# A fused attention, gated convolution and channel mix: reciprocals straight from PSUM for two pairs of six, and weights and vectors prepared at other places

## The chip, the core and the metric

One NeuronCore of one Trainium2 chip runs the kernel as one program. The metric is the device time of an execution in microseconds (us).

## What is computed

The batch is 4, there are 12 heads of 64, 448 positions, and the model width is 768. Three blocks follow each other:

```python
# attention with soft-capped scores
scores = cap * np.tanh(scale * np.matmul(q, k.transpose(0, 1, 3, 2)) / cap)
attn = np.exp(scores - max); attn = attn / (attn.sum(-1) + 1e-09)
x = np.matmul(attn, v)                        # then heads side by side: (4, 448, 768)
# gated causal convolution, 5 taps per channel
gate = 1 / (1 + np.exp(-gate_pre))            # gate_pre: sum of conv_w[k] * x shifted by k
x = gate * (x @ w_val) @ w_out
# channel mix
k = np.maximum(xk @ w_k, 0); v = k * k @ w_v  # xk, xr: x mixed with x one position before
out = 1 / (1 + np.exp(-(xr @ w_r))) * v
```

q, k, v, cap, mu_k and mu_r are float32; w_val, w_out, w_k, w_v, w_r and conv_w arrive as 64-bit floats.

## The kernel before

The work is cut by batch and by pair of heads. Two heads fill the 128 partitions, so there are 24 pairs, pair i being pair i % 6 of batch i // 6. Activations lie with channels on partitions and positions along the row (128 x 448). Each dense product is done in three matmuls: both operands are split into a high part and a remainder (`split_hi`, `split_lo`), and high x high, high x low and low x high are added in PSUM.

A pair goes through six pieces (`piece`): piece 0 makes two score tiles, their tanh and exp (`scores`, `exps`) and has GpSimd start adding up the exponentials (`add_up`); piece 1 multiplies the exponentials of the pair before with v (`pv`); pieces 2 and 3 turn q and k of the next pair (`qk_T`); piece 4 makes the other score tiles; piece 5 sums the exponentials of the pair before over the keys with a matmul against ones (`sums`, L294).

The sums have to be inverted and multiplied onto the pair's result `x_f`. In `sums`, ScalarE copies them out of PSUM (L296), a DMA spreads them over 128 partitions (7 columns), VectorE adds a small guard and inverts (`invert`, L300 and L301), a DMA writes them to DRAM, and `prep` loads them back as a full tile R (128 x 448, `load_R`). GpSimd multiplies (`divide`, L369). Then `prep` runs the five taps of the convolution over `x_f` (first tap on ScalarE L379, the other four on VectorE L385), and after the last pair of a batch a sigmoid over the whole gate (L389).

These steps are not issued at once. A clock of steps counts pieces and dense halves; `post(n, fn)` has fn issued n steps later. So the order of every engine's queue is written out by hand, and `in_order` keeps it:

```python
        post(2, lambda: dma(out=r, in_=rows[0::64]))
        post(4, invert)
        post(6, lambda: dma(out=rec_d[i]..., in_=r))
            post(8, load_R)
            post(11, divide)
            at(13 + k, tap, k)
            at(13 + TAPS, sigmoid)
```

All DMAs are issued by SyncE in the order of the program.

The weights arrive as 64-bit floats. `w_fetch` loads a unit (128 output columns), `narrow` makes 32-bit floats of it (one step on ScalarE, four on VectorE: L445 to L448), and `w_make` splits a half unit (three 128 x 128 blocks) into its two parts, and stores them to DRAM for the batches that follow. `w_ready` has the parts of the half four further on (LA = 4) loaded, or made if nobody made them before. The buffers of raw weights (tags x64 and wr) are two each.

The program has these stages. First, FIRST = 10 pairs run their pieces alone, with all six units of w_val narrowed between them (MAKE_IN = 46 is the tick by which they are to be done; units 3, 4, 5 and 0, 1 are split too). `vectors`, called ahead of pair 1, loads conv_w, mu_k and mu_r, narrows conv_w in five steps on VectorE and turns them with TensorE (L666) into per-channel columns. Then the layers val and out of batches 0 to 3 run (`first_stage`), each of six outputs in two halves of nine matmuls (`layer`, L631). Behind each half, `behind_first` issues pieces of the remaining pairs at a pace of 1.55 pieces a half in batches 0 and 1 and 3.0 after that; there, too, w_out's units are narrowed (batch 0) and w_r's (batch 1), and the x of the next batch is split (SPLIT_AT, `x_split`). In batch 3 and after it w_k and w_v are made resident, and r, k and v of all batches follow (`second_stage`). Behind all this stands a branch for a large cap, which these inputs don't take.

Of the kernel before, what the change touches and what calls it, by code (L numbers as in the profile page):

```python
# [8 lines left out]
F32 = mybir.dt.float32  # L9
F32R = mybir.dt.float32r  # L10
I32 = mybir.dt.int32
I64 = mybir.dt.int64
ACTF = mybir.ActivationFunctionType
ALU = mybir.AluOpType
# [2 lines left out]
DRAM = bass.MemoryType.DRAM  # L17


FIRST = 10  # L20

MAKE_IN = 46

PACE = (1.55, 1.55, 3.0)

SPLIT_AT = (14, 15, 16, 21, 22, 23)

# [6 lines left out]
LA = 4  # L34
# [12 lines left out]
def attention_gated_conv_channel_mix_kernel(  # L47
# [27 lines left out]
    nc = tc.nc  # L75
    B, H, S, D = q.shape
# [3 lines left out]
    NP = H // 2  # L80
# [60 lines left out]
    def dma(**kw):  # L141
        nc.sync.dma_start(**kw)  # L142
# [15 lines left out]
    def post(n, fn, *args):  # L158
        due.setdefault(steps[0] + n, []).append((fn, args))
# [30 lines left out]
    def load_v(i):  # L190
        b, hp = divmod(i, NP)
        vn = pools["raw"].tile([128, J, D], F32, tag="vn", name="vn")
        dma(
            out=vn,
            in_=v[b, 2 * hp:2 * hp + 2].rearrange("h s d -> (h s) d").rearrange("(j p) d -> p j d", p=128),
        )
        v_t[i] = (vn, vz[i % 2])
# [92 lines left out]
    def sums(i):  # L290
        acc = acc_t.pop(i)
        ps = ps_m.tile([128, S], F32, tag="sum", name="sum")
        for h in range(2):
            nc.tensor.matmul(ps[64 * h:64 * h + 64], lhsT=ones, rhs=acc[:, h], start=True, stop=True)  # L294
        rows = pools["x"].tile([128, S], F32, tag="xs", name="rows", bufs=1)
        nc.scalar.copy(rows, ps)  # L296
        r = pools["x"].tile([128, NS], F32, tag="rec", name="rec")

        def invert():
            nc.vector.tensor_scalar(r, r, guard, None, ALU.add)  # L300
            nc.vector.reciprocal(r, r)  # L301

        post(2, lambda: dma(out=r, in_=rows[0::64]))
        post(4, invert)
        post(6, lambda: dma(out=rec_d[i].rearrange("h s -> (h s)").rearrange("(p n) -> p n", n=NS), in_=r))
        prep(*divmod(i, NP))

    def shifted(i):
# [45 lines left out]


    again = [False]
    x_f, x_R, x_blk, gate_t, gated = {}, {}, {}, {}, set()

    def prep(b, hp):

        i = b * NP + hp
        at = (lambda t, fn, *args: fn(*args)) if again[0] else post

        def load_R():
            x_R[i] = pools["x"].tile([128, S], F32, tag="R", name="R")
            dma(out=x_R[i], in_=rec_d[i].unsqueeze(1).to_broadcast([2, 64, S]))

        def divide():
            nc.gpsimd.tensor_tensor(x_f[i], x_f[i], x_R.pop(i), ALU.mult)  # L369

        def tap(k):
            if hp == 0 and k == 0:
                gp = gr_p if b % 2 else pools["x"]
                gate_t[b] = gp.tile([128, KD, S], F32, tag="gr", name="gate", bufs=1)
            x, g = x_f[i], gate_t[b][:, hp]
            eng = turn(GATE[b], hp)
            w = vecT[:, hp, TAPS - 1 - k:TAPS - k]
            if k == 0:
                nc.scalar.activation(out=g, in_=x, func=ACTF.Copy, scale=w)  # L379
            elif eng is nc.gpsimd:  # L380
                y = pools["x"].tile([128, S], F32, tag="tap", name="tap", bufs=1)
                eng.tensor_scalar(y[:, k:], x[:, :S - k], w, 1.0, ALU.mult, ALU.mult)
                eng.tensor_tensor(g[:, k:], g[:, k:], y[:, k:], ALU.add)
            else:
                eng.scalar_tensor_tensor(g[:, k:], x[:, :S - k], w, g[:, k:], ALU.mult, ALU.add)  # L385

        def sigmoid():
            ga = gate_t[b].rearrange("p k s -> p (k s)")
            nc.scalar.activation(out=ga, in_=ga, func=ACTF.Sigmoid)  # L389
            gated.add((b, again[0]))  # L390

        if not again[0]:
            post(8, load_R)
            post(11, divide)
        if again[0] or b == 0:
            at(14, x_split, b, hp)
        for k in range(TAPS):
            at(13 + k, tap, k)
        if hp == KD - 1:
            at(13 + TAPS, sigmoid)  # L400

    def new_blk():
        return blk_p.tile([128, 2, S], F32R, tag="blk", name="blk")
# [1 line left out]
    def split_blk(src, hi_eng, lo_eng, wait=0):  # L405
        t = new_blk()
        split_hi(hi_eng, t[:, 0], src)
        if wait:
            post(wait, split_lo, lo_eng, t[:, 1], src, t[:, 0])
        else:  # L410
            split_lo(lo_eng, t[:, 1], src, t[:, 0])
        return t[:, 0], t[:, 1]

    def x_split(b, hp):
        x_blk[b, hp] = split_blk(x_f[b * NP + hp], nc.scalar, engines["PD"[hp % 2]], 0 if again[0] else 1)


# [232 lines left out]
                pend.append((b, o))  # L650

    def vectors():
        vec = pools["mk"].tile([128, DM], F32, tag="wr", name="vec")[0:8]
        if conv_w.dtype == I64:
            c64 = pools["mk"].tile([128, DM, 2], I32, tag="x64", name="c64")
            dma(out=c64[0:TAPS].rearrange("p n two -> p (n two)"), in_=conv_w.bitcast(I32))
        else:
            dma(out=vec[0:TAPS], in_=conv_w)
        dma(out=vec[TAPS:TAPS + 1], in_=mu_k.unsqueeze(0))
        dma(out=vec[TAPS + 1:TAPS + 2], in_=mu_r.unsqueeze(0))  # L660
        if conv_w.dtype == I64:
            for fn in narrow(c64[0:TAPS], vec[0:TAPS]):
                fn()
        pc = ps_m.tile([128, KD, 8], F32, tag="sum", name="pc")
        for o in range(KD):
            nc.tensor.transpose(  # L666
                pc[:, o, :TAPS + 2], vec[:TAPS + 2, o * 128:(o + 1) * 128], ident[:TAPS + 2, :TAPS + 2]
            )
        nc.vector.tensor_copy(vecT[:, :, :TAPS + 2], pc[:, :, :TAPS + 2])
        nc.vector.tensor_scalar(mu1, vecT[:, :, TAPS:TAPS + 2], -1.0, 1.0, ALU.mult, ALU.add)  # L670


    stage = ExitStack()
# [2 lines left out]
    dma(out=cap_c, in_=cap.to_broadcast([128, 1]))  # L676
    load_qk(1)
    load_v(0)
    make_identity(nc, ident)
    for p in prev:  # L680
        nc.vector.memset(p[:, 0:1], 0.0)
# [52 lines left out]

    first = len(nc.cur_bb.bb.instructions)
    ops = []
    order = (3, 4, 5, 0, 1, 2)[:KD]

    def make_val(j):
        o = order[j]  # L740
        ops.extend(w_wide("val", o, "ADDDD"))
        if j + 1 < len(order):
            w_fetch("val", order[j + 1])
        for a in range(2):
            if j < 3:
                ops.append(lambda a=a: w_make("val", o, a, nc.vector))
            elif 2 * o + a < LA:
                ops.append(lambda a=a: w_spl.update({2 * o + a: w_make("val", o, a, nc.vector)}))
        if j < 3:
            made.add(("val", o))  # L750
        if j + 1 < len(order):
            ops.append(lambda: make_val(j + 1))

    make_val(0)
    n_ops, n_done, ticks = 8 * len(order), 0, 0
    for i in range(FIRST):
        if i == 1:
            vectors()
        for p in pieces(i):
            piece(*p)  # L760
            ticks += 1
            while ops and n_done * MAKE_IN < ticks * n_ops:
                ops.pop(0)()
                n_done += 1
            step()
    while ops:
        ops.pop(0)()
    dense_from[0] = 0


# [4 lines left out]
    def behind_first(b):  # L775
        def behind(n):
            credit[0] += PACE[min(b, len(PACE) - 1)]
            while todo and credit[0] >= 1:
                piece(*todo.pop(0))
                credit[0] -= 1  # L780
                step()
            u = n // 2

            if b == 0 and KD <= u + 3 < 2 * KD:
                if n % 2 == 0:
                    wide.extend(w_wide("out", u + 3 - KD, "ADDDD"))
                    if u + 4 < 2 * KD:
                        w_fetch("out", u + 4 - KD)
                for _ in range(1 if n % 2 == 0 else len(wide)):
                    if wide:  # L790
                        wide.pop(0)()
            if b == 1 and u // 2 < KD:
                o = u // 2
                if n % 4 == 0:
                    wide.extend(w_wide("r", o, "ADDDD"))
                    if o + 1 < KD:
                        w_fetch("r", o + 1)
                if n % 4 < 2:
                    for _ in range(1 if n % 2 == 0 else len(wide)):
                        if wide:  # L800
                            wide.pop(0)()
                else:
                    w_make("r", o, n % 4 - 2, (nc.gpsimd, nc.vector)[n % 2])
                    made.add(("r", o))
            if b == B - 1:
                if n + 1 in XR_AT0:
                    mixed(0, XR_AT0.index(n + 1), 1)
                return lambda: res_step("val")
            elif n + 1 in SPLIT_AT and not again[0]:
                x_split(b + 1, SPLIT_AT.index(n + 1))  # L810
        return behind
# [100 lines left out]
```

## Time and profile before

| | |
|---|---|
| median of 3 runs | 879.13 us (877.95 to 880.84) |
| the profiled execution, its own time | 877.56 us |
| its span, from first to last instruction | 875.8 us |
| TensorE busy (mean granted clock 0.938) | 752.7 us, 86% of the span |
| VectorE, ScalarE, GpSimd busy | 480.0, 443.1, 343.6 us |

The profile is of one execution. PE is TensorE, DVE VectorE, ACT ScalarE, POOL GpSimd, SP SyncE, whose queue issues the DMAs. In the granted clock 1.00 is 2.4 GHz and 0.5 is 1.2 GHz. Idle time in front of an instruction is given with what ended it (`<-`). An engine takes its instructions strictly in order, so what stands behind a waiting instruction waits too. L631 is line 631 of the kernel. TensorE's busy time contains matmuls at half clock and gaps in the pipeline, so it isn't the least time that its work needs.

### The profile page before, as it was taken

What the parts mean: (1) busy time and instruction counts of PE and PEld (TensorE: products, weight loads), DVE (VectorE), ACT (ScalarE), POOL (GpSimd) and SP (SyncE); (2) the same over time, 40 slices, a digit from 0 to 9 for tenths busy, and PEclk for the clock granted to TensorE, in tenths of its full rate; (3) what the DMA queues carried; (4) which work ended last, traced back from release to release, by engine and by line L of the source; (5) the groups of instructions that cost most, each with busy time, mean ns of one, the idle gap of its engine ahead of it and who ended that gap; (6) DMA issues with size and microseconds to landing.
All of it is one profiled execution on the core that took longest, in us unless ns stands there. A gap on an engine that the chain in (4) does not pass through costs nothing.

```text
span 875.8 us, 10699 instructions
## 1 busy us (share of the span) xinstructions
PE 752.7 (86%) x3798; PEld 583.8 (67%) x3798; DVE 480.0 (55%) x653; ACT 443.1 (51%) x673; POOL 343.6 (39%) x259
## 2 busy tenths in 40 slices
PE   3676689869789898779899977888999999999996
PEld 2333345536456655545789756768999999999995
DVE  3577887759945746464525756886423332333310
ACT  4475869647575757676232445543443343335311
POOL 2296777636744636576023646774000000000000
PEclk8687879979889999999989999999999999999999
DMA  7264533564647577754668898333720390145001
GB/s 177 66 178 133 148 91 90 140 192 146 205 154 242 182 206 231 236 166 130 209 219 305 292 311 302 108 118 99 229 74 21 85 286 15 43 124 168 1 21 47
DMA packets 148029, 135.50 MB, mean 155 GB/s; under 512 B 78071, under 2 KB 127223, under 8 KB 147966
## 3 DMA queue, kind: packets, MB, share of 16 engines
q1 hardware_dynamic: 147966, 134.72, 51.4%
q8 instruction: 32, 0.52, 0.2%
q14 instruction: 31, 0.25, 0.1%
HBM read 109.35 MB, written 25.25 MB: 154 GB/s over the span
## 4 chain that ended last, share of the span: by engine, by line
PE 45%; DVE 16%; DMA 16%; ACT 10%; issue 6%; POOL 4%; SPq 2%; POOLq 0%; ACTq 0%; DVEq 0%
PE psd L631 37%; PE pv L286 3%; DMA rec<-rows 3%; DVE wr L447 3%; DMA recd<-rec 3%; PE s L244 3%; DVE gate L385 3%; ACT t L246 2%; DVE wr L446 2%; ACT t L253 2%; SPq L142 2%; DMA of<-out 2%; DVE wr L448 1%; DMA wp<-pdout 1%; DMA R<-recd 1%
## 5 line engine op out<-in xcount | busy, mean ns | idle before, releaser
L631 PE MATMUL psd<-blk,wp 128*128 128x448 f32 x1296 | 292.3, 381 | 20.9 <-ACT r L568 6.3
L631 PEld LDWEIGHTS psd<-blk,wp 128*128 128x128 f32 x1296 | 246.6, 194 | 66.5 <-issue 21.3
L631 PE MATMUL psd<-blk,wv 128*128 128x448 f32 x576 | 124.6, 372 | 1.3 <-ACT blk L170 1.1
L170 ACT CAST blk<-f 128x448 fp32r<-128x448 f32 x104 | 59.0, 567 | 128.5 <-DVE f L592 52.8
L631 PE MATMUL psd<-blk,wk 128*128 128x448 f32 x576 | 118.5, 366 | 4.3 <-DVE f L576 4.2
L385 DVE SCALAR_TENSOR_TENSOR gate<-xf,vecT,gate 128x445 f32<-128x445 f32 (+2 forms) x96 | 95.0, 992 | 41.3 <-ACT gate L379 40.7
L631 PEld LDWEIGHTS psd<-blk,wk 128*128 128x128 f32 x576 | 107.9, 188 | 14.3 <-DVE f L576 5.8
L631 PEld LDWEIGHTS psd<-blk,wv 128*128 128x128 f32 x576 | 107.9, 190 | 10.5 <-ACT blk L170 1.4
L175 DVE TENSOR_TENSOR blk<-f,blk 128x448 fp32r<-128x448 f32 x104 | 76.3, 733 | 40.9 <-ACT blk L170 40.8
L271 POOL TENSOR_TENSOR acc<-acc,t 128x896 f32<-128x896 f32 x24 | 54.5, 2271 | 73.5 <-ACT t L253 73.4
L244 PE MATMUL s<-qh,kh 64*128 64x448 f32 x192 | 46.3, 474 | 39.9 <-DVE kh L172 23.9
L246 ACT ACTIVATE t<-s 128x896 f32<-128x896 f32 x72 | 64.0, 917 | 32.0 <-PE s L244 32.0
L253 ACT ACTIVATE t<-t 128x1792 f32<-128x1792 f32 (+1 forms) x48 | 72.5, 1511 | 1.2
L268 POOL TENSOR_TENSOR acc<-t 128x896 f32<-128x896 f32 x24 | 54.2, 2258 | 45.2 <-ACT t L253 27.5
L286 PE MATMUL pv<-t,vn 128*64 128x448 f32 x288 | 70.0, 627 | 0.1
L274 POOL TENSOR_TENSOR acc<-acc,t 64x448 f32<-64x448 f32 x48 | 64.2, 1338 | 3.6
L592 DVE SCALAR_TENSOR_TENSOR f<-of,vecT,prev 128x448 f32<-128x448 f32 x48 | 33.5, 698 | 49.3 <-ACT prev L590 45.8
L244 PEld LDWEIGHTS s<-qh,kh 64*128 64x128 f32 x192 | 19.9, 199 | 59.0 <-issue 19.2
L445 POOL TENSOR_SCALAR wr<-wr 128x384 f32<-128x384 f32 (+1 forms) x28 | 53.5, 1909 | 11.7 <-ACT wr L443 11.6
L576 DVE TENSOR_TENSOR f<-psd,kr 128x448 f32<-128x448 f32 x32 | 19.9, 622 | 61.8 <-ACT kr L574 61.8
L369 POOL TENSOR_TENSOR xf<-xf,R 128x448 f32<-128x448 f32 x24 | 29.5, 1230 | 61.3 <-DMA R<-recd 60.4
L447 DVE SCALAR_TENSOR_TENSOR wr<-x,wr 128x768 int32<-128x768 int32 (+2 forms) x46 | 48.7, 1058 | 1.4
(79 smaller groups left out, 881.1 us busy)
## 6 DMA issues: line engine op xcount, KB each, us to landing
wp<-pdr SPq DMA_DIRECT2D x48, 384.0 KB
wp<-pdval SPq DMA_DIRECT2D x42, 384.0 KB
wp<-pdout SPq DMA_DIRECT2D x36, 384.0 KB
of<-out SPq DMA_DIRECT2D x48, 224.0 KB
x<-in_moe_w_k_dram SPq DMA_DIRECT2D x16, 384.0 KB
x<-in_moe_w_v_dram SPq DMA_DIRECT2D x12, 512.0 KB
qn<-in_q_dram SPq DMA_DIRECT2D x48, 112.0 KB
kn<-in_k_dram SPq DMA_DIRECT2D x48, 112.0 KB
```

Of the source, the lines that this page charges most:

```text
L170: eng.copy(dst, src)
L175: eng.tensor_tensor(dst, src, hi.bitcast(F32), ALU.subtract)
L244: nc.tensor.matmul(ps[:, h], lhsT=a[r, keys[h]], rhs=x[r], start=(m == 0), stop=(m == 2))
L246: nc.scalar.activation(out=t_t[i][:, at:at + 2], in_=ps, func=ACTF.Tanh, scale=reg_t)
L253: nc.scalar.activation(out=a, in_=a, func=ACTF.Exp, scale=reg_e)
L268: eng.tensor_tensor(acc_t[i], t[:, 0:2], t[:, 2:4], ALU.add)
L271: eng.tensor_tensor(acc, acc, t[:, 4:6], ALU.add)
L274: eng.tensor_tensor(acc[r, h], acc[r, h], t[r, 6], ALU.add)
L286: nc.tensor.matmul(ps[64 * h:64 * h + 64], lhsT=w, rhs=t[:, at], start=(n == 0), stop=(n == 3))
L385: eng.scalar_tensor_tensor(g[:, k:], x[:, :S - k], w, g[:, k:], ALU.mult, ALU.add)
L447: lambda: D.scalar_tensor_tensor(mi, hw, -(1 << 30), mi, ALU.bitwise_and, ALU.bitwise_or),
L631: nc.tensor.matmul(ps, lhsT=lhsT, rhs=x[xp], start=(kk == 0 and m == 0), stop=(kk == kb - 1 and m == 2),)
```

## The change

Constants: FIRST 10 to 8, MAKE_IN 46 to 40, and the pace (batch 0, batch 1, later) from 1.55, 1.55, 3.0 to 1.5, 1.5, 1.35. For the last two pairs of each batch the sums are inverted at full width, from PSUM, without ScalarE's copy and the three DMAs, and the steps behind them come sooner; for the other pairs some steps are posted one or two later. In the first stage only units 0 to 2 of w_val are narrowed (0 and 1 split); units 3 to 5 follow behind the halves of batch 0's val, ahead of w_out's. The loads of the vectors are issued at the start, their narrowing is spread over the pieces of pair 0, and their turning comes after piece 4 of pair 1.

```diff
-FIRST = 10
-MAKE_IN = 46
-PACE = (1.55, 1.55, 3.0)
+FIRST = 8
+MAKE_IN = 40
+PACE = (1.5, 1.5, 1.35)
...
             nc.tensor.matmul(ps[64 * h:64 * h + 64], lhsT=ones, rhs=acc[:, h], start=True, stop=True)
+        if i % NP >= NP - 2:
+
+            def invert():
+                R = x_R[i] = pools["x"].tile([128, S], F32, tag="R", name="R")
+                nc.vector.tensor_scalar(R, ps, guard, None, ALU.add)
+                nc.vector.reciprocal(R, R)
+
+            post(1, invert)
+            prep(*divmod(i, NP), early=True)
+            return
...
-        post(4, invert)
-        post(6, lambda: dma(out=rec_d[i].rearrange("h s -> (h s)").rearrange("(p n) -> p n", n=NS), in_=r))
+        post(5, invert)
+        post(7, lambda: dma(out=rec_d[i].rearrange("h s -> (h s)").rearrange("(p n) -> p n", n=NS), in_=r))
...
-            post(8, load_R)
-            post(11, divide)
+            if not early:
+                post(9, load_R)
+            post(3 if early else 13, divide)
         if again[0] or b == 0:
-            at(14, x_split, b, hp)
+            at(5 if early else 15, x_split, b, hp)
         for k in range(TAPS):
-            at(13 + k, tap, k)
+            at(4 + (k + 1) // 2 if early else 15 + k, tap, k)
         if hp == KD - 1:
-            at(13 + TAPS, sigmoid)
+            at(4 + (TAPS + 1) // 2 if early else 15 + TAPS, sigmoid)
...
     load_v(0)
+    vec_ops, vec_turned = vectors()
     make_identity(nc, ident)
...
-    order = (3, 4, 5, 0, 1, 2)[:KD]
+    order = range(3)
...
         for a in range(2):
-            if j < 3:
-                ops.append(lambda a=a: w_make("val", o, a, nc.vector))
-            elif 2 * o + a < LA:
+            if 2 * o + a < LA:
                 ops.append(lambda a=a: w_spl.update({2 * o + a: w_make("val", o, a, nc.vector)}))
-        if j < 3:
-            made.add(("val", o))
...
     for i in range(FIRST):
-        if i == 1:
-            vectors()
         for p in pieces(i):
             piece(*p)
+            if i == 0 and vec_ops:
+                for _ in range(2):
+                    if vec_ops:
+                        vec_ops.pop(0)()
+            if p == (1, 4):
+                vec_turned()
...
     while ops:
         ops.pop(0)()
+    w_fetch("val", len(order))
     dense_from[0] = 0
...
-            if b == 0 and KD <= u + 3 < 2 * KD:
+            units = [(nm, o) for nm in ("val", "out") for o in range(KD)]
+            if b == 0 and u + 3 < 2 * KD:
                 if n % 2 == 0:
-                    wide.extend(w_wide("out", u + 3 - KD, "ADDDD"))
+                    wide.extend(w_wide(*units[u + 3], "ADDDD"))
                     if u + 4 < 2 * KD:
-                        w_fetch("out", u + 4 - KD)
+                        w_fetch(*units[u + 4])
```

The rest of the diff splits `vectors` into its loads, the list of narrowing steps that it returns, and the turning (`turned`), and keeps a set of the pairs that have been divided.

## Rows read from the trace of the kernel before

**Rows 1.** Busy us by stage: PE, PEld, DVE, ACT, POOL, granted clock, DMA share, GB/s.

```profile
31.00:143.00 112.00, 87.07 (x470) 43.63 (x469) 88.28 (x106) 79.56 (x106) 79.00 (x58) 0.82 0.48 130
143.00:204.00 61.00, 49.75 (x266) 33.10 (x264) 40.03 (x51) 39.85 (x53) 31.73 (x27) 0.92 0.53 142
204.00:269.00 65.00, 54.71 (x280) 35.45 (x276) 48.97 (x54) 45.81 (x69) 41.24 (x30) 0.89 0.56 173
269.00:388.00 119.00, 103.50 (x546) 66.63 (x544) 70.53 (x93) 77.43 (x112) 66.71 (x53) 0.96 0.73 220
```

**Rows 2.** Timeline, PE: first matmuls of batches 0, 2 (halves 0, 4) and 3.

```profile
142.94 1.30 PE L631 MATMUL psd<-blk,wp 128*128 128x448 f32 x5
...
388.24 1.08 PE L631 MATMUL psd<-blk,wp 128*128 128x448 f32 x4
...
414.54 0.88 PE L631 MATMUL psd<-blk,wp 128*128 128x448 f32 x3
...
459.19 0.98 PE L631 MATMUL psd<-blk,wp 128*128 128x448 f32 x4
```

**Rows 3.** The chain that ended last, at full clock: start us, us, what.

```profile
161.20 0.97 PE sum L294 x4
...
397.94 1.41 PE s L244 x12
399.35 3.16 PE pv L286 x16
...
621.01 55.94 PE psd L631 x276
```

**Rows 4.** Timeline of the start: start us, us, instruction, idle before it.

```profile
16.37 0.56 DVE L445 TENSOR_SCALAR wr<-wr 128x768 f32<-128x768 f32 x1 [7.78 <-ACT wr L443]
...
19.16 0.62 DVE L175 TENSOR_TENSOR kl<-psq,kh 128x448 fp32r<-128x448 f32 x1
...
24.36 0.33 SPq L142 DMA_DIRECT2D c<-in_moe_conv_w_dram  x1
...
30.23 0.81 PE L666 MATMUL pc<-ident,vec 7*128 7x7 f32 x6 [16.06 <-DVE vec L448]
30.97 0.74 PE L244 MATMUL s<-qh,kh 64*128 64x448 f32 x2
```

**Rows 5.** Timeline from 170 to 188 us.

```profile
170.72 0.60 PE L211 MATMUL psq<-ident,qn 112*128 112x112 f32 x4
...
176.28 1.61 SPq L142 DMA_DIRECT2D x<-in_moe_w_out_dram  x2
...
186.19 0.89 ACT L443 ACTIVATE wr<-x 128x768 f32<-128x768 f32 x1 [11.60 <-DMA x<-in_moe_w_out_dram]
...
187.94 0.74 PE L244 MATMUL s<-qh,kh 64*128 64x448 f32 x2 [8.19 <-ACT t L246]
```

**Rows 6.** DVE's instructions on weights (tile wr) in two stretches: busy us, clock, DMA.

```profile
31.00:143.00 112.00, 38.18 (x30) 0.82 0.48 130
143.00:388.00 245.00, 59.58 (x60) 0.93 0.64 188
```

**Rows 7.** Groups of the whole span: busy us, mean ns of one, idle before.

```profile
L300 DVE TENSOR_SCALAR rec<-rec,guard 128x7 f32<-128x7 f32 x24 | 13.8, 575 | 37.0 <-DMA rec<-rows 37.0
L301 DVE RECIPROCAL rec<-rec 128x7 f32<-128x7 f32 x24 | 4.8, 201 | 0.8
L684 DVE RECIPROCAL inv_c<-cap_c 128x1 f32<-128x1 f32 x1 | 0.2, 165 | 0.0
L385 DVE SCALAR_TENSOR_TENSOR gate<-xf,vecT,gate 128x445 f32<-128x445 f32 (+2 forms) x96 | 95.0, 992 | 41.3 <-ACT gate L379 40.7
L369 POOL TENSOR_TENSOR xf<-xf,R 128x448 f32<-128x448 f32 x24 | 29.5, 1230 | 61.3 <-DMA R<-recd 60.4
L389 ACT ACTIVATE gate<-gate 128x2688 f32<-128x2688 f32 x4 | 9.8, 2449 | 0.1
```

**Rows 8.** What PE waited for from 143 to 388: us, times, longest.

```profile
PE sum L294 <- DVE ql L175: 11.0, 6, 3.6
```

More of the change, by code (lines that the diff above doesn't have):

```diff
@@ L356, in attention_gated_conv_channel_mix_kernel, with prep @@
     again = [False]
-    x_f, x_R, x_blk, gate_t, gated = {}, {}, {}, {}, set()
-    def prep(b, hp):
+    x_f, x_R, x_blk, gate_t, gated, divided = {}, {}, {}, {}, set(), set()
+    def prep(b, hp, early=False):
         i = b * NP + hp
@@ L369, in divide @@
             nc.gpsimd.tensor_tensor(x_f[i], x_f[i], x_R.pop(i), ALU.mult)
+            divided.add(i)
         def tap(k):
@@ L414, in x_split @@
     def x_split(b, hp):
+        assert again[0] or b * NP + hp in divided
         x_blk[b, hp] = split_blk(x_f[b * NP + hp], nc.scalar, engines["PD"[hp % 2]], 0 if again[0] else 1)
@@ L653, in vectors @@
         vec = pools["mk"].tile([128, DM], F32, tag="wr", name="vec")[0:8]
+        ops = []
         if conv_w.dtype == I64:
@@ L656, in vectors @@
             dma(out=c64[0:TAPS].rearrange("p n two -> p (n two)"), in_=conv_w.bitcast(I32))
+            ops = narrow(c64[0:TAPS], vec[0:TAPS])
         else:
@@ L660, in vectors, with turned @@
         dma(out=vec[TAPS + 1:TAPS + 2], in_=mu_r.unsqueeze(0))
[L661 to L670, printed above, removed]
+        def turned():
+            pc = ps_m.tile([128, KD, 8], F32, tag="sum", name="pc")
+            for o in range(KD):
+                nc.tensor.transpose(
+                    pc[:, o, :TAPS + 2], vec[:TAPS + 2, o * 128:(o + 1) * 128], ident[:TAPS + 2, :TAPS + 2]
+                )
+            nc.vector.tensor_copy(vecT[:, :, :TAPS + 2], pc[:, :, :TAPS + 2])
+            nc.vector.tensor_scalar(mu1, vecT[:, :, TAPS:TAPS + 2], -1.0, 1.0, ALU.mult, ALU.add)
+        return ops, turned
     stage = ExitStack()
```

## The prediction

> **What bounds the kernel now.** I read the busy time by stage first, with the stages cut where TensorE starts the dense layers of a batch [rows 1, 2], then TensorE's own prices from the chain that ended last [rows 3], then the stalls one by one. The dense layers of batch 0 start at 142.9 us, those of batch 2 at 388.2, those of batch 3 at 459.2 [rows 2]. The span is 875.8 us, so batch 3 and all that follows take 416.6 us; the change touches nothing there, and its whole effect is read as when batch 3 starts.
>
> At full clock a dense matmul takes 55.94 / 276 = 0.203 us, so a half (9 matmuls) takes 1.82 and a batch's 24 halves 43.8. A pair's attention on TensorE is two score pieces of 1.41, the product with v 3.16, the sums 0.97 [rows 3] and two transposed tiles of 0.60 [rows 5]: 8.15 us, or 1.36 for each of its six pieces. Now compare with the time used.
> - Attention alone: pairs 1 to 9 run from 31 to 143, that is 12.4 us a pair, where TensorE needs 8.15. No engine is full: VectorE is busy 88 of 112 us, TensorE 87 at 0.82 of its clock, ScalarE and GpSimd 80 and 79 [rows 1].
> - Batches 0 and 1: 48 halves and 48 x 1.55 = 74.4 pieces, least 87.6 + 101.2 = 188.8 us, used 245.3. That is 0.77 of the time; a piece costs (245.3 - 87.6) / 74.4 = 2.12 us.
> - Batch 2: four halves carry the last 12 pieces and take 26.3 us, against a least of 7.3 + 14.7 (three score pieces, two products, three sums, two tiles), a share of 0.835; the batch takes 71.0 [rows 2].
>
> So the time before batch 3 is not one engine's load: it is in-order queues that wait for each other, and TensorE idles most while there is no dense work to fill in. Some stalls have one address. From about 14 to 30 us TensorE stands 16.06 us in front of the turning of the vectors, which waits for five VectorE steps on data whose DMA was issued only at 24.4; pair 1's scores stand behind it though their input was done at 19.8 [rows 4]. At 188 us it idles 8.19 us because ScalarE waits 11.6 us for the first weights of w_out, whose fetch was issued at 176.3, right ahead of the step that reads them [rows 5].
>
> **The change part by part.**
> *Vectors first.* Three small DMA issues (0.33 us the first) move ahead of the loads of pair 2, v of pair 1 and val's first weights on SyncE; the five VectorE steps move into pair 0, where VectorE idles 7.78 us before its first narrowing [rows 4], so they cost nothing (without that cover, at most the 5.9 us from the issue to the turning). The turning moves behind pair 1's scores. Pair 1 then starts when VectorE has split its keys, about 20 instead of 31: **-11** (ends 0, if ScalarE and GpSimd only move their waiting, and -12). Next in line is VectorE itself.
>
> *FIRST 8, three units of val ahead.* Two pairs leave the first stage; seven remain after pair 0. VectorE's load there: 88.3 in all, 38.2 of it on weights (five units narrowed, ten halves split) [rows 6], 50.1 other. Weights fall to two units and four halves, 2/5: 15.3. The other work loses two pairs' splits of q and k (four steps of 0.62 each [rows 4], -5) and three small reciprocals (-2), and gains two wide ones (+7, below), since both early pairs and all six pairs' taps still lie in this stage: 50. Together 65 us for seven pairs, 9.3 a pair against 9.8: about as loaded as before, so I keep 12.4 a pair: 7 x 12.4 = 87 instead of 112, **-25** (ends: 65 if VectorE ran without a gap, -47; 94 if the wide reciprocals came on top, -18). Batch 0 starts at 107.
>
> *Batches 0 and 1.* Pace 1.5 for 1.55: 2.4 pieces fewer, -5. Val's units 3 to 5 are now narrowed and split here. One unit cost VectorE 59.6 / 12 = 5.0 us here, the split of one half in it [rows 6]: +15; GpSimd gets three splits. Six weight parts less are read back, with the raw weights read here instead, so DMA is even. The fetch of w_out's first unit now runs two halves ahead and its 8.2 us go; the same cold fetch moves to val's unit 3, issued about one piece and a half before its reader: I take 3 for it, -5 (ends 0, -8).
>
> *The reciprocals.* For pairs 4 and 5 of each batch the row copy, three DMAs and a small reciprocal fall away; VectorE does an addition from PSUM on 128x448 (0.62 like the split of k from PSUM [rows 4]) and a reciprocal on 448 columns, which the trace lacks. Nearest: 201 ns for 7 columns, 165 for one [rows 7], 6 ns a column, so 0.165 + 447 x 0.006 = 2.85 us; ends 0.62 (a plain step of this size) and 2.85, and I take 2.85, it is the same operation. Less the 0.78 of the small steps it replaces: +2.7 us each, four in batches 0 and 1: +11.
> The Trainium skill, VectorE: DVE Perf Modes, section "First, the fixed hardware budget", speaks against this part: a reciprocal is an iterative divide with a repeat count of 8. At eight cycles a column of VectorE's 0.96 GHz (the Trainium skill, Trainium Kernel Development and Optimization, section Quick Reference, has the clock) this would be an estimated 3.7 us and the eight of them 7 us more of VectorE work, some 2 us on the sum; the trace's slope of 6 ns is a little under that and decides here.
>
> VectorE's added 15 + 11 = 26 us in these batches: it was busy 159 of 245 us [rows 1] and becomes 185. I let a third reach the end, +9 (ends 0 and 26). On GpSimd the division moves up to three steps after the sums; it waits for the reciprocal, and the adding up of the next exponentials queues behind it. Two steps of some 2 us each lie between, about the 3.5 us that VectorE needs, so I charge nothing more; without that cover it would be some 3 us a pair. The sums' bank is held until VectorE's addition instead of ScalarE's copy; its next user comes three pieces later. The other pairs' splits and taps come one or two steps later, which costs nothing as long as pair 5 ends the batch: its sigmoid is due 7 steps behind its sums, before 18.
> What the early way gives back: TensorE waited 11.0 us for q's low half behind VectorE's queue [rows 8], where the small reciprocals wait for their DMA. A third of the pairs skip that, the others get one to two steps more: -6 (ends 0, -11). Together -5 - 5 + 9 - 6 = **-7**; batches 0 and 1 take 238.
>
> *Batch 2.* Of 98 pieces 72 are done; 26 remain, at 1.35 a half, until its 20th half. Their least is 8 score pieces, 5 products, 5 sums and 6 tiles: 35.5 us, and 43.8 dense: 79.3. The share lies between the 0.77 of batches 0 and 1, which also made weights, and 1 where dense runs alone [rows 3]; the nearest is 0.835, with more attention to a half than this will have. I take 0.88: 90 us against 71.0, **+19** (ends +8, +32).
>
> *The end of batch 2.* Pair 23's chain was hidden by 20 dense halves. Now it is reciprocal 2.85, division 1.23, four taps of 0.99 and the sigmoid's 2.45 [rows 7], some 11 us with its first steps, and four halves (7.3) and two outputs of batch 3 (7.3) cover it: **+2** (ends 0, +10).
>
> Sum: -11 - 25 - 7 + 19 + 2 = -22. The profiled execution took 877.6 us (span 875.8), the median is 879.1; I take the difference off the median: **857**. About 0.3% (2.6 us) is what a measurement of this kernel can tell from no change.
>
> **The rivals.**
> *VectorE becomes the bound (slower).* Place: its in-order queue from batch 0 to batch 2, where val's product, which the out layer needs, stands behind wide reciprocals and narrowings. Then all 26 us land (+17), the waits behind it stay (+6), and batch 2 runs at batch 0's share, 43.8 + 50.6 = 94.4 of 126, 0.75, so 79.3 / 0.75 = 106 (+16): 896. It decides once these exceed 22. For: the ready work of this queue already makes TensorE wait [rows 8]. Against: VectorE is at 65% there, at 76% after. Chance 0.10.
> *Cold fetches.* Val's unit 3 and w_out's first each stall TensorE as [rows 5] show: 16.4 - 8.2 instead of -5, +13: 870. Against: units fetched two halves ahead show no such wait before. Chance 0.11.
> *All waits go.* The rest of the 11.0 (5 more) and batch 2 at TensorE's least (-11): 841. Chance 0.15.
> *It does not do what it says.* The hole at 14 to 30 is refilled by ScalarE's and VectorE's own queues (+11) and pair 23's chain is exposed (+10): 878, no change. Chance 0.07.
>
> **Chances and range.** My forecast has 0.54; 0.03 are left for other mixes, 0.02 of them faster and 0.01 slower. Faster: 0.54 + 0.15 + 0.11 + 0.02 = 0.82; same 0.07; slower 0.11. From 840 to 877 lie the forecast with its bounds, the fetches and the case without waits, 0.8.
>
> **What would show it.** Right: batch 0's first dense matmul near 107, batch 2's near 345, batch 3's near 437, and 417 us from there to the end; eight reciprocals of 128x448 near 2.9 us and sixteen small ones; no wait at the turning of the vectors. Wrong: a batch 2 over 100 us, TensorE waiting for VectorE's val product, ScalarE waiting for val's weights in batch 0, or a gap at batch 3's first outputs behind the sigmoid.

## The result, and the profile after

The changed kernel takes 857.89 us (median of 4 runs, 856.46 to 863.07) against 879.05 of the kernel before in the same measurement: a ratio of 0.9766, with a 95% interval of 0.9738 to 0.9795. The forecast was 857. The profiled execution took 858.22 us, its span 856.4. So the sum was right; its terms were less so. The three places at which the forecast cuts the time, first dense matmul of batch 0, of batch 2 and of batch 3, from TensorE's timeline of the changed kernel:

```profile
103.71 0.84 PE L644 MATMUL psd<-blk,wp 128*128 128x448 f32 x3 [2.95 <-DVE ql L175]
...
349.04 0.87 PE L644 MATMUL psd<-blk,wp 128*128 128x448 f32 x3
...
434.64 1.19 PE L644 MATMUL psd<-blk,wp 128*128 128x448 f32 x5
```

Against [rows 2]:

| stretch | before | after | measured | forecast |
|---|---|---|---|---|
| start to batch 0's first dense matmul | 142.9 | 103.7 | -39.2 | -36 |
| batches 0 and 1 | 245.3 | 245.3 | 0.0 | -7 |
| batch 2 | 71.0 | 85.6 | +14.6 | +19 |
| batch 3 to the end | 416.6 | 421.8 | +5.2 | +2 |
| span | 875.8 | 856.4 | -19.4 | -22 |

Busy time by stage (columns as in [rows 1]), cut at the same places as there:

```profile
20.00:103.00 83.00, 64.15 (x360) 30.40 (x358) 67.47 (x71) 55.67 (x71) 64.16 (x49) 0.86 0.46 119
103.00:166.00 63.00, 50.04 (x252) 31.47 (x254) 49.69 (x60) 42.85 (x60) 36.05 (x28) 0.93 0.49 146
166.00:235.00 69.00, 55.34 (x280) 35.83 (x276) 52.89 (x61) 40.01 (x60) 39.81 (x31) 0.89 0.59 185
235.00:349.00 114.00, 99.07 (x530) 64.47 (x528) 74.41 (x90) 75.04 (x109) 62.96 (x50) 0.97 0.70 216
```

In the first stage VectorE (the third sum) is busy 67 of 83 us, 0.81, as against 0.79 before: the stage got shorter at the same load, as the forecast has it. In batches 0 and 1 VectorE has 177 us instead of 159, in the same 245 us; the forecast had 185. The unchanged sum of the two batches hides two changes: batch 0 takes 131.4 us instead of 126.1, batch 1 takes 113.9 instead of 119.1.

The hole at the start is gone. The turning of the vectors (L681) comes after pair 1's last scores and waits for nothing; pair 1's scores start at 17.4 us, where the forecast had 20 and the kernel before 31 [rows 4]. From the timeline of the changed kernel:

```profile
17.33 0.62 DVE L175 TENSOR_TENSOR kl<-psq,kh 128x448 fp32r<-128x448 f32 x1
17.44 0.74 PE L244 MATMUL s<-qh,kh 64*128 64x448 f32 x2 [3.24 <-DVE kh L172]
...
27.20 0.53 PE L681 MATMUL pc<-ident,vec 7*128 7x7 f32 x6
```

The new and the remaining steps of the reciprocals, and the division behind them, from the groups of the whole span:

```profile
L379 POOL TENSOR_TENSOR xf<-xf,R 128x448 f32<-128x448 f32 x24 | 29.3, 1225 | 13.4 <-DVE R L300 10.9 <-DMA R<-recd 1.7
...
L300 DVE RECIPROCAL R<-R 128x448 f32<-128x448 f32 x8 | 23.6, 2953 | 0.3
...
L299 DVE TENSOR_SCALAR R<-sum,guard 128x448 f32<-128x448 f32 x8 | 5.4, 676 | 1.6 <-PE sum L294 1.6
...
L311 DVE RECIPROCAL rec<-rec 128x7 f32<-128x7 f32 x16 | 3.2, 201 | 0.5
```

The wide reciprocal takes 2.953 us, where 2.85 was worked out from [rows 7]. GpSimd's division waited 61.3 us for its operand before, nearly all of it for the DMA, and waits 13.4 now.

Last, what TensorE waited for in batches 0 and 1 (us in total, times, longest), to be read beside [rows 8]. First two more rows of the kernel before (143 to 388 us):

```profile
PE s L244 <- ACT t L246: 12.8, 3, 8.2
PE psq L211 <- ACT xf L288: 6.4, 4, 2.7
```

Then the changed kernel (103 to 349 us):

```profile
PE s L244 <- ACT t L246: 17.7, 11, 4.1
PE psq L211 <- ACT xf L288: 14.3, 7, 5.6
PE psd L644 <- DVE blk L175: 4.7, 1, 4.7
PE psd L644 <- DVE ql L175: 2.9, 1, 2.9
PE sum L294 <- DVE ql L175: 1.4, 3, 0.6
```

The 11.0 us in front of the sums have become 1.4. But TensorE now waits 32.0 us for ScalarE's tanh and copies instead of 19.2 (8.2 of those were the one cold fetch of [rows 5], which is gone), and 4.7 us for VectorE's split of pair 5 in batch 0's second half. The 2.9 us for `ql` stand in front of the first dense matmul, so they belong to the stage before. Where the forecast's -7 went is taken up below.

### The profile page after: what moved, and what is told of

Read it like the earlier page. It is cut to its first block, busy times and chain, and to the rows that moved or that the text cites. A ratio compares the mean times of both kernels' runs of the same rounds, so it can differ in the third digit from the quotient of the medians.

```text
span 856.4 us, 10628 instructions
## 1 busy us (share of the span) xinstructions
PE 752.1 (88%) x3798; PEld 578.8 (68%) x3798; DVE 496.3 (58%) x646; ACT 441.9 (52%) x669; POOL 344.7 (40%) x262
## 4 chain that ended last, share of the span: by engine, by line
PE 44%; DVE 23%; ACT 12%; DMA 8%; POOL 7%; issue 5%; SPq 1%; POOLq 0%; ACTq 0%; DVEq 0%
PE psd L644 37%; DVE gate L396 7%; DVE wr L460 3%; PE pv L286 3%; PE s L244 2%; ACT t L253 2%; ACT t L246 2%; DVE wr L459 2%; DMA of<-out 2%; POOL acc L271 2%; DVE wr L461 2%; POOL acc L274 2%; DMA x<-in_moe_w_k_dram 1%; POOL xf L379 1%; ACT t L249 1%
## 5 line engine op out<-in xcount | busy, mean ns | idle before, releaser
L644 PE MATMUL psd<-blk,wp 128*128 128x448 f32 x1296 | 298.5, 383 | 26.1 <-DVE blk L175 9.9
L644 PEld LDWEIGHTS psd<-blk,wp 128*128 128x128 f32 x1296 | 246.5, 196 | 73.5 <-issue 21.5
L396 DVE SCALAR_TENSOR_TENSOR gate<-xf,vecT,gate 128x447 f32<-128x447 f32 (+2 forms) x96 | 88.7, 936 | 33.2 <-ACT gate L390 32.3
L271 POOL TENSOR_TENSOR acc<-acc,t 128x896 f32<-128x896 f32 x24 | 52.5, 2189 | 108.3 <-ACT t L253 108.2
L286 PE MATMUL pv<-t,vn 128*64 128x448 f32 x288 | 67.1, 606 | 0.0
L618 ACT COPY on<-pso 112x512 f32<-112x512 f32 x24 | 14.1, 586 | 68.1 <-PE pso L616 67.8
```

Of the source, the lines that this page charges most:

```text
L271: eng.tensor_tensor(acc, acc, t[:, 4:6], ALU.add)
L286: nc.tensor.matmul(ps[64 * h:64 * h + 64], lhsT=w, rhs=t[:, at], start=(n == 0), stop=(n == 3))
L644: nc.tensor.matmul(ps, lhsT=lhsT, rhs=x[xp], start=(kk == 0 and m == 0), stop=(kk == kb - 1 and m == 2),)
```

## The experiments

Ratios are to the kernel before on the same chip, with 95% intervals; the changed kernel stands at 0.9766. Where a batch starts, in us from the span's start, is when its first dense matmul starts in the run's trace. A trace is one execution: in five runs with the same instructions up to there, batch 0 starts at 103.1 to 105.6 us, and in the four of them that are the same to the end of batch 1, batches 0 and 1 take 245.1 to 246.2. Differences of 2 us between stages therefore say little.

**Vectors alone**, on the kernel before:

```diff
+    vec_ops, vec_turned = vectors()        # loads, right behind load_v(0)
-        if i == 1:
-            vectors()
+            if i == 0 and vec_ops: ...     # two steps behind each piece of pair 0
+            if p == (1, 4):
+                vec_turned()
```

> The kernel before with the vectors loaded first, narrowed in pair 0 and turned after pair 1's piece 4, and nothing else of the change. If the hole at the start is worth what the prediction took, pair 1 starts 11 us sooner and all behind it too: 868 us. Rival: ScalarE's and VectorE's queues only move their waiting, the first stage is filled by weights anyway: 877 to 880.

869.07 us, 0.9892 (0.9864 to 0.9920). Batch 0 starts at 131.4 instead of 142.9, 11.5 us sooner, and batch 3 at 447.0 instead of 459.2. The hole was worth about what it showed, and nothing behind it filled it again.

**The early way alone**, on the kernel before (wide reciprocals and sooner steps for pairs 4 and 5 of a batch, other posts as before):

```diff
+        if i % NP >= NP - 2:
+            post(1, invert)                # VectorE, 128x448
+            prep(*divmod(i, NP), early=True)
+            return
```

> The kernel before with the wide reciprocals and the sooner steps for the last two pairs of each batch, and nothing else of the change (10 pairs first, the paces of before). If the small reciprocals' way through three DMAs is what makes TensorE wait in batches 0 and 1 and delays batch 2, 870 to 874. If the wide reciprocals alone bring nothing and only allow the first stage to end two pairs sooner, 876 to 882. Rival, they cost what they weigh on VectorE: 887 or more.

886.00 us, 1.0076 (1.0052 to 1.0101): 0.8% slower, next to the rival's 887. Batches 0 and 1 do gain, 239.0 us instead of 245.3, the size that the forecast put on the waits saved there; the wait in front of the sums falls from 11.0 to 5.8. The first stage loses more than that: batch 0 starts at 156.7 instead of 142.9. The timelines of this run show how, first VectorE's, then TensorE's:

```profile
101.31 2.95 DVE L300 RECIPROCAL R<-R 128x448 f32<-128x448 f32 x1
...
133.74 0.74 PE L244 MATMUL s<-qh,kh 64*128 64x448 f32 x2 [10.93 <-DVE kh L172]
```

Between 98 and 139 us VectorE has no gap: two reciprocals, the early pairs' taps squeezed into three steps, the late taps of the pairs before and val's narrowings stand in one queue, and the split of k, which TensorE needs for the next pair's scores, stands behind them. TensorE idles 10.93 us in one place.

**All six units of val in the first stage**, on the changed kernel:

```diff
-    order = range(3)
+    order = (3, 4, 5, 0, 1, 2)[:KD]
...
-            if b == 0 and u + 3 < 2 * KD:
+            if b == 0 and KD <= u + 3 < 2 * KD:
```

> The changed kernel with all six units of val narrowed in the first stage (3, 4, 5 split too), as before the change, and the first unit of w_out fetched at its end. By VectorE's load the first stage grows by 23 us of weights at its share of 0.79, some 25 to 29, and batch 0 gives 5 back, as the run without those steps showed: 878 to 882. Rival, eight pairs hide the weights in VectorE's idle time: 858 or less.

860.39 us, 0.9781 (0.9744 to 0.9818). The first stage grows by 12.5 us (batch 0 starts at 116.3), not by 25, and batches 0 and 1 give back 9.9 (235.4 instead of 245.3). So the 23 us of weights are not charged at VectorE's busy share; the stage grows by about half of them. Where val's units are made hardly matters to the sum at eight pairs: the intervals overlap widely.

**Without the wide reciprocals**, on the changed kernel:

```diff
                 nc.vector.tensor_scalar(R, ps, guard, None, ALU.add)
-                nc.vector.reciprocal(R, R)
```

> The changed kernel without its eight wide reciprocals (the pairs' results are multiplied by the sums, so the inversion is left out); 8 x 2.95 = 23.6 us less on VectorE. If a third of VectorE's added work lands on the end, as the prediction took, 850 us. Rival, VectorE's queue is the bound and all of it lands: 834. Rival, the reciprocals are covered except at the ends of the first stage and of batch 2: 854 to 858.

852.53 us, 0.9697 (0.9665 to 0.9728): 5 us less for 23.6 us of VectorE's work, a quarter rather than a third. The gain isn't in batches 0 and 1, which take 247.0 us here. It lies where the second rival has it, at the ends of stages: batch 0 starts sooner, and batch 3 to the end takes 419.9 instead of 421.8, which by itself is within what traces differ by. From TensorE's timeline of this run:

```profile
97.05 0.55 PE L294 MATMUL sum<-acc,ones 128*64 128x448 f32 x2
97.52 0.68 PE L643 MATMUL psd<-blk,wp 128*128 128x448 f32 x2
```

The dense layers follow the sums without a wait, 6.2 us sooner than at 103.71. In the changed kernel TensorE waits 2.95 us there, with VectorE's queue ahead of it so:

```profile
99.48 2.95 DVE L300 RECIPROCAL R<-R 128x448 f32<-128x448 f32 x1
102.35 0.56 DVE L172 CAST qh<-psq 128x448 fp32r<-128x448 f32 x1
102.94 0.62 DVE L175 TENSOR_TENSOR ql<-psq,qh 128x448 fp32r<-128x448 f32 x1
```

By the kernel, in the first stage the transposed q and k take their PSUM buffers from the two of tag "d", which the dense layers use too. So the first dense matmul waits until VectorE has split pair 8's q, and that stands behind pair 5's reciprocal. The two reciprocals of the first stage, 5.9 us, land whole as far as one trace can tell. The four of batches 0 and 1, which the forecast charged with 11 us of VectorE's work and nearly 4 us of the end, cost nothing that shows, although with a sooner start of batch 0 the two effects aren't fully apart.

**Val's units 3 to 5 not narrowed**, on the changed kernel (ScalarE's step stays):

```diff
-                    wide.extend(w_wide(*units[u + 3], "ADDDD"))
+                    made_ops = w_wide(*units[u + 3], "ADDDD")
+                    wide.extend(made_ops[:1] if u < 3 else made_ops)
```

> The changed kernel without the four VectorE steps that narrow units 3 to 5 of val in batch 0 (those steps are left out, the weights of three units are not the right ones); some 11 us less on VectorE. A third lands: 854. Rival, it is ScalarE's queue, whose splits wait for these steps, that holds TensorE in batch 0: 848 or less, and ScalarE's wait for the narrowed weights shrinks by 8 us or more between 104 and 166 us. Rival, no influence: 858.

853.69 us, 0.9728 (0.9691 to 0.9765); the interval still touches the changed kernel's. Batches 0 and 1 take 239.7 us, 5.6 less, 5.2 of it in batch 0 (126.2 for 131.4). The whole gains 4.2. So a third to a half of the 11 us removed reaches the end, near the first expectation. ScalarE's wait for narrowed weights between 104 and 166 us was only 4.1 us to begin with, so it cannot shrink by 8 (it goes to nothing): this rival falls. What holds ScalarE in batch 0 is another wait, which this run leaves as it was. The row with the most of it, from 105 to 232 us of this run:

```profile
ACT wr L456 <- POOL wp L175: 15.7, 7, 3.7
```

A raw unit is narrowed into one of two buffers, and ScalarE's first step on the next unit waits until GpSimd has split the last half of the unit that had the buffer before. In the changed kernel this wait is 15.3 us in six times from 103 to 235; the longest such wait in the kernel before's batch 0 was for a DMA. Another buffer was not tried.

**The early pairs' split ahead of their taps**, on the changed kernel:

```diff
-            at(5 if early else 15, x_split, b, hp)
+            at(4 if early else 15, x_split, b, hp)
-            at(4 + (k + 1) // 2 if early else 15 + k, tap, k)
+            at(5 + (k + 1) // 2 if early else 15 + k, tap, k)
```

> The changed kernel with the early pairs' split one step sooner and their taps and sigmoid one step later. If TensorE's waits at batch 0's first two halves (2.95 and 4.67 us) come from pair 5's split standing behind taps in VectorE's queue, they shrink by some 4 us: 854. Rival, they come from the reciprocal and the division in front: no change, 858. Rival, the gate is then late for val's first product: 861.

859.22 us, 0.9785 (0.9758 to 0.9812): no change in the sum, but not in its parts. The wait of 4.67 in the second half is gone, so it did come from the order of VectorE's queue. The wait ahead of the first half stays (3.15), since it is for q's split behind the reciprocal and not for pair 5's split. The first four halves start at 105.67, 110.55, 116.10 and 124.18 us, against 103.71, 107.89, 120.67 and 123.93: the third is 4.6 us sooner, and the fourth has lost it again. TensorE's waits in this run, ahead of the fourth half and at the start of batch 2:

```profile
123.50 1.01 PE L211 MATMUL psq<-ident,kn 112*128 112x112 f32 x4 [5.30 <-ACT xf L288]
...
354.59 0.74 PE L244 MATMUL s<-qh,kh 64*128 64x448 f32 x2 [6.81 <-ACT t L246]
```

In the changed kernel these are 0.79 and 2.75. At both places ScalarE's copy or tanh stands behind the sigmoid of a batch, whose taps come one step later here. So batch 0 becomes 4.2 us shorter (127.2), batch 2 3.9 longer (89.5): with this much work left on VectorE at a border, either order has TensorE wait for one of the two.

**A faster pace in batch 2**, on the changed kernel:

```diff
-PACE = (1.5, 1.5, 1.35)
+PACE = (1.5, 1.5, 1.6)
```

> The changed kernel with a pace of 1.6 instead of 1.35 from batch 2 on, so that the last piece is issued behind the 17th half and not the 20th. If the 5 us that batch 3 and what follows take longer than before come from pair 23's chain, which ends too near to batch 3, they shrink to 1 or 2 and batch 2 stays within 2 us: 855. Rival, batch 2 with more attention to a half loses what the end gains: 858 to 861.

857.77 us, 0.9756 (0.9715 to 0.9797): no change, though the attention ends three halves sooner. Batch 2 takes 85.2 us, batch 3 to the end 423.1. TensorE still waits in batch 3's first halves, since the split of pair 23 keeps its place behind the 23rd half.

**The same with a sooner split**:

```diff
+SPLIT_LAST = (14, 15, 16, 17, 18, 20)
...
-            elif n + 1 in SPLIT_AT and not again[0]:
-                x_split(b + 1, SPLIT_AT.index(n + 1))
+            at = SPLIT_LAST if b == B - 2 else SPLIT_AT
+            if n + 1 in at and not again[0]:
+                x_split(b + 1, at.index(n + 1))
```

> The changed kernel with a pace of 1.6 from batch 2 on and the split of batch 3's x there behind the halves 14, 15, 16, 17, 18, 20 instead of 14, 15, 16, 21, 22, 23. In the run with the pace alone TensorE still waited 2.45 us at the start of batch 3, since pair 23's split stood behind ten taps and the sigmoid. If that order is the cause of batch 3's lost time, the wait goes and batch 3 to the end takes 417 to 418 us instead of 422: 854. Rival, the tail's load on VectorE only comes out elsewhere in batch 3: 857 to 858.

856.75 us, 0.9753 (0.9726 to 0.9779), beside 0.9772 of the changed kernel measured with it (below): the intervals overlap, so it isn't shown to be better. The last stretch takes 420.5 us, not 417. The wait only changed its name; timeline of this run:

```profile
436.77 2.44 ACT L402 ACTIVATE gate<-gate 128x2688 f32<-128x2688 f32 x1
439.12 0.51 ACT L578 COPY f<-psd 128x448 f32<-128x448 f32 x1
...
439.69 3.57 PE L646 MATMUL psd<-blk,wp 128*128 128x448 f32 x16 [3.06 <-ACT f L578]
```

Batch 3's sigmoid waits in ScalarE's queue for the last tap. Behind it stands the copy of batch 2's last output, which has to free a PSUM buffer before TensorE can go on.

**The changed kernel again**, unchanged:

> The changed kernel as it is, beside the two others on the same chip: 858, its ratio to before 0.976 as in its own measurement.

859.70 us, 0.9772 (0.9747 to 0.9796).

**How many pairs first, and the paces.** Three runs of the changed kernel:

```diff
-FIRST = 8
+FIRST = 9
```

> The changed kernel with 9 pairs first instead of 8. A pair costs some 12 us in the first stage and its six pieces some 10 us in batch 2, so 860. Rival, batch 2 gives the whole of 14 us back, since its end then comes early enough to hide pair 23's chain: 854. Rival, batch 2 gives nothing back: 868.

```diff
-FIRST = 8
+FIRST = 10
-PACE = (1.5, 1.5, 1.35)
+PACE = (1.55, 1.55, 3.0)
```

> The changed kernel with 10 pairs first and the paces of before (1.55, 1.55, 3.0): vectors first, wide reciprocals and val's three units in batch 0 stay. From the prices measured so far, 879 less 10 for the vectors, plus 7.6 for the early way, less 2.5 for val's units: 874, so that the two pairs moved and the paces are worth 16 us. Rival, the price of one pair from 9 to 8 (1.5 us) goes on as it is: 861. Rival, with val's units out of the first stage the early way costs nothing: 866.

```diff
-FIRST = 8
+FIRST = 10
```

> The changed kernel with 10 pairs first and its own paces (1.5, 1.5, 1.35), so that against the run with 10 pairs and the old paces only the paces differ. If the 16 us between that run and the one with 9 pairs come from the pair that leaves the first stage, the paces give back 2.4 pieces at 2.1 us in batches 0 and 1, lose about as much in batch 2: 870 to 876. Rival, the paces are what counts, and the number of pairs ahead hardly does: 858 to 863.

| run | us, ratio | batch 0 starts | batches 0, 1 take | batch 2 takes | the rest takes |
|---|---|---|---|---|---|
| 10 pairs, old paces | 875.25, 0.9961 (0.9943 to 0.9979) | 133.9 | 249.4 | 73.5 | 416.7 |
| 10 pairs, new paces | 866.06, 0.9854 (0.9830 to 0.9877) | 132.6 | 239.8 | 75.8 | 415.0 |
| 9 pairs, new paces | 859.38, 0.9770 (0.9739 to 0.9802) | 123.0 | 242.6 | 75.7 | 416.7 |
| 8 pairs, new paces (the change) | 857.89, 0.9766 (0.9738 to 0.9795) | 103.7 | 245.3 | 85.6 | 421.8 |

With 10 pairs and the old paces 874 was expected, and it is 875. With the new paces both the expectation (870 to 876) and its rival (858 to 863) fell: it is 866. The paces give 9 us, all in batches 0 and 1. There the waits for the low halves of q and k nearly go; TensorE's waits with the old paces (134 to 383 us), then with the new ones (133 to 372):

```profile
PE s L244 <- DVE kl L175: 8.3, 4, 5.1
PE sum L294 <- DVE ql L175: 7.3, 5, 2.8
...
PE sum L294 <- DVE ql L175: 1.9, 3, 0.9
PE s L244 <- DVE kl L175: 0.4, 2, 0.2
```

In their place the waits for ScalarE's tanh and copies grow from 17.4 to 32.2 us. In all, TensorE's busy time in these batches falls by 5.8 us and its idle time by 3.9; why the paces give more than their pieces cost isn't shown.

The pair from 10 to 9 gives 7. Batch 2 takes its six pieces at no cost, where with 10 pairs TensorE waits 5.4 us in one place, with a granted clock of 0.50 from 426 to 430 us behind it, and with 9 pairs has no such wait and a granted clock of 1.00 throughout. The pair from 9 to 8 gives nothing that can be measured, since the 19 us that the first stage loses come back as 3 in batches 0 and 1, 10 in batch 2 and 5 behind it. The 860 expected for 9 pairs was met, but with 19 us for the pair and not 12.

One comparison is missing: the vectors first and the new paces on the kernel before, with 10 pairs and without the early way. The vectors alone stand at 869 and the paces gave 9, so how much of the change needs the wide reciprocals isn't shown.

## Why the prediction was right, and where its terms were not

*The start, -11: right.* Alone it measured 11.5 us at batch 0's start and a ratio of 0.9892, 9.5 us.

*The pairs, -25: right in size.* From pair 1's scores (17.4) to batch 0 it is 86.3 us, where 87 was forecast from the unchanged price of a pair. The reason given, that VectorE is about as loaded as before, holds too (0.81). What the forecast did not say is how the parts depend on each other here. The early way alone costs this stage 13.7 us. With val's three units out (10 pairs, old paces) batch 0 starts at 133.9, only 2.5 later than with the vectors alone, so most of that cost goes when the units go. At eight pairs the units put back cost 12.5, and the stage's two reciprocals 6.2. With eight or nine pairs first the early way could not just be left out for comparison: by the posts, batch 0's sigmoid would be issued behind the step that reads the gate.

*Batches 0 and 1, -7: wrong, 0.* The runs with 10 pairs allow a sum beside the forecast's. Each figure is the difference between two traces:

| step | forecast | measured | between |
|---|---|---|---|
| early way | -6 | -6.3 | before, early way alone |
| val's units here, fetches, later posts | -5 + 9 | +10.4 | early way alone, 10 pairs with old paces (vectors first too) |
| paces | -5 | -9.6 | 10 pairs, old and new paces |
| two pairs fewer ahead | nothing | +5.5 | 10 pairs with new paces, the change |

- The early way gave what was forecast, by the wait that was named: in front of the sums 5.8 of the 11.0 us are left with it. That only 1.4 are left in the changed kernel goes with the paces, which gave 9.6 us where the forecast counted only their 2.4 pieces at 2.1 us.
- The cold fetch went without a successor. ScalarE waits for no DMA in front of val's unit 3 or w_out's first.
- VectorE's +9 was in part in the wrong place: val's narrowing costs 5.6 here, the four reciprocals nothing that shows, but the two of the first stage 6.2. No run splits the +10.4 further, in which the later posts lie too.
- The missing term is what two pairs fewer ahead cost in these batches, and with it the entry of batch 0. The prediction followed the last pair's chain into batch 3 but not pair 5's into batch 0, though both have lost their distance. From the timeline of the changed kernel:

```profile
106.25 6.47 DVE L396 SCALAR_TENSOR_TENSOR gate<-xf,vecT,gate 128x446 f32<-128x446 f32 x6
112.64 1.55 DVE L175 TENSOR_TENSOR blk<-xf,blk 128x448 fp32r<-128x448 f32 x1
...
114.25 1.11 PE L644 MATMUL psd<-blk,wp 128*128 128x448 f32 x2 [4.67 <-DVE blk L175]
```

  In the second half TensorE waits 4.67 us for pair 5's split, which stands behind six taps on VectorE. With 9 or 10 pairs first there is no such wait. Together with the 2.95 us ahead of the first half, which fall into the stage before, this is the backlog at the border.
- The longer waits for ScalarE's tanh and copies do not explain the miss. They come with the new paces, 32.2 us with 10 pairs as against 32.0 in the changed kernel, and with these paces the stretch became shorter. The weights that wait in ScalarE's queue for a buffer which GpSimd still reads are seen in the trace; that they cost anything at the end isn't shown by a run.

*Batch 2, +19: too high, +14.6.* A share of 0.88 was taken; 79.3 / 85.6 is 0.93, with a single wait of 2.7 us. The attention disturbs the dense layers less here than in the piece-heavy halves at pace 3.0, and pace 1.6 gives the same; what makes the difference isn't shown. The 71.0 of before are no clean measure either: there TensorE waited 4.64 us in one place for weights of out, and its granted clock was 0.50 from 438 to 442 us, behind that wait.

*The end, +2: too low, +5.2.* The mechanism was named; the cover was counted too generously. VectorE's, TensorE's and ScalarE's timelines of the changed kernel as batch 3 begins:

```profile
437.53 0.61 DVE L175 TENSOR_TENSOR blk<-xf,blk 128x448 fp32r<-128x448 f32 x1
440.68 0.62 DVE L175 TENSOR_TENSOR blk<-xf,blk 128x448 fp32r<-128x448 f32 x1
...
438.20 1.49 PE L644 MATMUL psd<-blk,wp 128*128 128x448 f32 x6 [1.33 <-DVE blk L175]
441.36 4.33 PE L644 MATMUL psd<-blk,wp 128*128 128x448 f32 x20 [1.67 <-DVE blk L175]
447.14 3.15 PE L644 MATMUL psd<-blk,wp 128*128 128x448 f32 x14 [1.46 <-DVE f L572]
...
442.69 1.28 ACT L400 ACT_TABLE_LOAD   x1 [6.05 <-DVE gate L396]
443.98 2.45 ACT L400 ACTIVATE gate<-gate 128x2688 f32<-128x2688 f32 x1
```

TensorE waits once for pair 21's split, which stands in VectorE's queue behind pair 23's reciprocal and taps, once for pair 23's own, and once for val's first product, which waits for the gate: 4.5 us, beside the 5.2. The forecast let two outputs of batch 3 cover the chain; but the x of pairs 21 to 23 is read already in the second half of the first output. Batch 3's two layers take 59.0 us instead of 52.4. The two runs that moved these waits, with a faster pace and a sooner split, did not get the 5 us back, so what each wait costs isn't shown. With 9 or 10 pairs first the stretch takes 415.0 to 416.7, as before.

The errors of +7, -4 and +3 against -3 at the start nearly cancel, which is luck, not insight. The same holds within batches 0 and 1. Of the rivals, VectorE as the bound and the exposed tail both exist, in small: the first at the borders and in batch 0, the second with half of the 10 us that it was given. Two of the signs of being wrong came too, in small: ScalarE waits 4.1 us for narrowed weights between 104 and 166 us, and TensorE 1.46 us at batch 3's first output, behind the sigmoid.

The Trainium skill (VectorE: DVE Perf Modes, "First, the fixed hardware budget") gives a reciprocal a repeat count of 8, and no time. The prediction's estimate from it, eight cycles a column, was 3.7 us; here it takes 2.953, so the slope of [rows 7] was the better guide.

## What to carry to other kernels

When work is moved closer to the stage that reads it, follow its last chain into the next stage at every border, not only at the last one: here 2.95 and 4.67 us of waiting stood at the border to batch 0 and 4.5 at that to batch 3, while reciprocals in mid-stage cost nothing that showed. Changing the order at such a border moved the waits and left the sum. A shortcut that trades a DMA round trip for work on a busy engine can lose alone (0.8% slower here) and cost far less once load is taken off that engine, so price the two together; whether the better schedule needed it was not measured here. And price an added step by what stands behind it in its queue: 23.6 us of reciprocals cost 5, and the two with TensorE's first dense matmul waiting behind them cost all of their 5.9.

## What the runs showed of the hardware

A reciprocal on VectorE takes 0.165 us for 1 column, 0.201 for 7 and 2.953 for 448, the same within 2 ns in all eight: (2953 - 201) / 441 = 6.2 ns a column, while the addition from PSUM on the same 448 columns takes 0.676. Here the small rows gave a fair price of the long one (2.85), with the slope taken and not the mean per column.

Two waits of TensorE in batch 2 were followed by the lower clock. In the kernel before it stood idle for 4.64 us until 438.75 us, and the granted clock was 0.50 (1.2 GHz) from 438 to 442; in the run with 10 pairs and the new paces it stood idle for 5.36 us until 426.87, and the clock was 0.50 from 426 to 430.
